# A fused retention and channel-mix kernel: eight key loads on one queue and a new hand-written order

## The chip, the cores and the metric

The kernel runs on one core of a Trainium2 chip. The metric is the device time of one execution in microseconds; the median of the runs is what two kernels are compared by. The engines are named as in the profile: PE (TensorE matrix products; PEld its weight loads), DVE (VectorE), ACT (ScalarE), POOL (GpSimd), SP (SyncE). ACTq, SPq and POOLq are the sequencers of those engines, which also issue DMAs.

## What is computed

Two layers, one after the other, for 4 batches, 8 heads, 768 positions and head dimension 64. The first is a recurrent retention layer with a decay per head:

```python
gamma = 1.0 - 2.0 ** (-5.0 - np.arange(H))
for t in range(S):
    state = gamma * state + einsum('bhd,bhe->bhde', k[:, :, t], v[:, :, t])
    y[:, :, t] = scale * einsum('bhd,bhde->bhe', q[:, :, t], state)
```

Its result, heads side by side (512 values for each position), is the x of the second layer, a channel mix of each position with the one before it:

```python
xk = mu_k * x + (1.0 - mu_k) * x_prev
xr = mu_r * x + (1.0 - mu_r) * x_prev
k = np.maximum(xk @ w_k, 0.0)            # 512 -> 1024
v = k * k @ w_v                          # 1024 -> 512
r = 1.0 / (1.0 + np.exp(-(xr @ w_r)))    # 512 -> 512
return (r * v).astype(np.float32)
```

Inputs and output are float32.

## The kernel before

The positions are cut into 24 chunks c of 128 (six to a batch) for the retention layer and into 12 blocks m of 256 (three to a batch, chunks 2m and 2m+1) for the channel mix. The work is written as pieces, and a long string, ORDER, names every piece in the order in which the program is emitted. There is no other scheduler: each engine runs its own pieces in the order of that string and waits at each for what it needs. The kernel's loop is only this:

```python
for piece in ORDER.split():
    name, *args = piece.split(".")
    pieces[name](*map(int, args))
```

The pieces of chunk c, with the engine that runs them:

- q.c, k.c, v.c: loads of one chunk, 256 KB of float32 in the source. q and v are cast to float16 on the way and always stand in POOL's queue. k stays float32, and its queue is the c-th entry of LOADED_BY, or SP from chunk 8 on.
- ks: the scaling of k by powers of the decay. ks.0.0, ks.0.1, ks.1.0, ks.1.1 (pairs 0 and 1, one chunk each) run on the engine that SCALED_BY names; ks.2 to ks.11 scale two chunks at once on POOL.
- T.c: transposes of q and ks on PE (16 products). TC.c: their copy to float16 on ACT.
- A.c: scores on PE. M.c.0, M.c.1: the causal mask on DVE.
- S.c: update of the state on PE. SE.c: its copy, on ACT for even c, on DVE for odd c.
- Y.c: the chunk's result on PE. YE.c: its decay and copy into xT on DVE.

The pieces of block m: dx.m, the difference to the previous position (on DVE for blocks 0 and 1, there written dx.m.0 and dx.m.1; on POOL for the others); xk.m.j and xr.m.j, the mixtures, on DVE; G.m.g, a quarter of the product with w_k, on PE, and K.m.g, relu and square, on ACT; R.m.t, the product with w_r, on PE, and RS.m.t, the sigmoid, on ACT; V.m.t.p, halves of the product with w_v, on PE; O.m.t, the last product, on DVE; out.m.t, the store, on SP. wk.0, wk.1, wr, wv.0, wv.1 load the weights (1 MB of float32 each, cast to float16) and muk, mur the two mixing vectors; pw.0 and pw.1 make tables of decay powers on DVE.

Chunks are loaded into tiles of two chunks each. There are five such tiles for q, five for v and two for k, so that k.4 can only be loaded when chunks 0 and 1 have been scaled, k.6 after chunks 2 and 3, k.8 after ks.2, and so on. The two choices that the change touches beside ORDER are used here:

```python
def load_k(c):
    eng = getattr(nc, LOADED_BY[c] if c < len(LOADED_BY) else "sync")
    load(k, K32, "k32", F32, eng, c)

eng = nc.gpsimd if c is None else getattr(nc, SCALED_BY[2 * n + c])
if eng is nc.scalar:
    for h in range(H):
        eng.activation(out=KS[n][:, c, h], in_=K32[n][:, c, h], func=AF.Copy, scale=gk[:, c, h : h + 1])
else:
    w = gk[:, e, :, None].to_broadcast([P, e.stop - e.start, H, D])
    eng.tensor_tensor(out=KS[n][:, e], in0=K32[n][:, e], in1=w, op=ALU.mult)
```

Of the kernel before, what the change touches and what calls it, by code (L numbers as in the profile page):

```python
# [28 lines left out]
M.7.1 K.1.3 S.6 xk.2.2 V.0.0.0 q.11 M.7.0 SE.6 Y.6 xk.2.0 q.9 V.0.1.1 xk.2.3 xr.2.0 V.1.0.1 q.8
xk.2.1 V.0.0.1 xr.2.1 v.8 O.1.0 Y.7 YE.6 out.1.0 G.2.2 k.13 YE.7 T.9 k.10 O.0.1 dx.3 S.7 k.11 TC.9  # L30
T.8 SE.7 k.12 G.2.3 TC.8 O.0.0 G.2.0 v.9 xr.2.2 K.2.2 xr.2.3 A.9 A.8 v.10 M.9.1 V.1.1.0 K.2.0
xk.3.2 q.12 S.8 xk.3.3 V.1.1.1 xk.3.1 K.2.3 q.10 xk.3.0 G.2.1 O.1.1 q.13 SE.8 G.3.1 M.8.1 ks.5
K.2.1 M.9.0 G.3.2 M.8.0 R.2.0 K.3.2 xr.3.2 ks.6 k.14 S.9 Y.9 k.15 SE.9 T.11 Y.8 YE.9 TC.11 G.3.3
YE.8 v.11 k.17 RS.2.0 T.10 xr.3.0 out.0.1 A.11 dx.4 k.16 TC.10 S.10 M.11.1 V.2.0.0 M.11.0 SE.10
G.3.0 xr.3.1 q.15 K.3.3 xk.4.2 A.10 xr.3.3 V.2.0.1 v.12 xk.4.3 K.3.0 M.10.0 T.12 v.13 R.2.1 xk.4.0
TC.12 q.14 xk.4.1 T.13 M.10.1 K.3.1 Y.11 q.23 xr.4.1 G.4.3 YE.11 q.16 RS.2.1 Y.10 xr.4.3 TC.13
V.2.1.0 YE.10 G.4.1 K.4.3 dx.5 A.13 A.12 K.4.1 M.13.0 V.3.1.0 ks.7 M.13.1 S.12 V.2.1.1 O.2.0 SE.12
M.12.1 G.4.0 out.2.0 ks.8 O.2.1 G.4.2 K.4.0 xr.4.0 out.2.1 S.13 k.19 T.14 q.21 T.15 k.20 xk.5.1
V.3.0.0 k.21 TC.15 M.12.0 v.20 out.0.0 R.3.0 xr.4.2 xr.5.1 v.14 Y.13 xr.5.2 RS.3.0 Y.12 q.17 YE.13
V.3.0.1 TC.14 xr.5.3 v.15 V.3.1.1 YE.12 K.4.2 T.16 xk.5.3 dx.6 V.4.1.0 SE.13 TC.16 O.3.0 R.3.1  # L40
xk.5.0 V.4.1.1 v.19 RS.3.1 xk.5.2 A.15 O.3.1 A.14 R.4.1 M.14.1 ks.10 M.15.1 G.5.1 RS.4.1 M.14.0
R.4.0 xk.6.2 G.5.2 v.18 k.22 RS.4.0 xk.6.3 k.18 xk.6.0 S.14 v.16 xk.6.1 T.17 SE.14 V.4.0.0 O.4.1
q.18 K.5.1 M.15.0 out.4.1 S.15 Y.14 q.19 out.3.0 SE.15 G.5.3 out.1.1 K.5.2 YE.14 G.6.0 xr.6.2
TC.17 xr.6.3 G.5.0 K.5.3 A.16 A.17 M.16.0 V.4.0.1 K.5.0 ks.9 M.16.1 G.6.1 M.17.1 S.16 xr.5.0 K.6.1
G.6.3 v.23 xr.6.0 Y.15 xr.6.1 K.6.0 v.17 Y.16 YE.15 R.5.0 YE.16 K.6.3 dx.7 R.6.1 M.17.0 SE.16
V.5.0.0 O.4.0 v.21 xk.7.3 RS.5.0 T.21 xk.7.2 S.18 T.18 q.20 xk.7.0 SE.18 T.19 V.5.0.1 q.22 TC.18
G.6.2 v.22 O.5.0 TC.19 xr.7.3 S.19 out.5.0 Y.17 RS.6.1 xk.7.1 k.23 R.5.1 SE.19 TC.21 out.3.1 R.6.0
xr.7.2 K.6.2 YE.17 G.7.2 xr.7.1 dx.8 G.7.1 K.7.2 A.19 A.18 RS.6.0 V.6.0.0 M.18.0 ks.11 RS.5.1
M.18.1 G.7.3 K.7.1 M.19.0 T.20 xk.8.2 V.5.1.0 TC.20 xk.8.3 xr.7.0 G.7.0 M.19.1 V.6.0.1 K.7.0
xk.8.0 A.20 A.21 M.20.0 R.7.1 K.7.3 M.21.0 V.5.1.1 RS.7.1 xk.8.1 M.21.1 S.20 Y.18 SE.20 G.8.0  # L50
O.6.0 M.20.1 Y.19 R.7.0 O.5.1 YE.18 out.5.1 G.8.1 RS.7.0 xr.8.3 K.8.0 Y.20 YE.19 V.7.1.0 xr.8.1
dx.9 K.8.1 xr.8.2 G.8.3 G.8.2 K.8.3 V.6.1.0 xr.8.0 K.8.2 YE.20 Y.21 S.21 xk.9.1 V.7.1.1 xk.9.0
xr.9.2 V.6.1.1 YE.21 T.23 xk.9.2 dx.10 V.8.0.0 O.7.1 TC.23 O.6.1 R.8.0 out.7.1 SE.21 out.6.1 T.22
RS.8.0 out.4.0 V.8.1.0 xk.10.0 TC.22 out.6.0 xk.10.3 R.8.1 xk.9.3 xr.10.1 A.22 RS.8.1 A.23 M.22.1
V.8.1.1 M.23.1 G.9.0 M.23.0 S.22 xk.10.1 K.9.0 V.7.0.0 O.8.1 G.9.2 xk.10.2 SE.22 xr.9.1 V.7.0.1
xr.10.0 K.9.2 M.22.0 G.9.1 xr.9.0 O.7.0 G.10.0 K.9.1 out.7.0 Y.22 Y.23 K.10.0 V.8.0.1 YE.23 YE.22
G.10.3 O.8.0 G.9.3 K.10.3 xr.10.2 G.10.2 xr.9.3 xr.10.3 K.9.3 dx.11 G.10.1 R.9.1 K.10.1 R.9.0
xk.11.1 RS.9.1 xk.11.0 V.9.1.0 K.10.2 xk.11.3 xr.11.1 V.9.0.0 xk.11.2 RS.9.0 V.9.1.1 V.9.0.1 O.9.1
G.11.2 out.9.1 O.9.0 out.8.0 xr.11.2 R.10.0 K.11.2 out.8.1 xr.11.3 G.11.0 xr.11.0 G.11.3 K.11.0
G.11.1 RS.10.0 V.10.0.0 K.11.3 R.10.1 K.11.1 V.10.0.1 R.11.1 RS.10.1 O.10.0 V.10.1.0 out.10.0  # L60
RS.11.1 V.11.1.0 V.10.1.1 V.11.1.1 O.10.1 V.11.0.0 out.10.1 O.11.1 out.9.0 R.11.0 out.11.1
V.11.0.1 RS.11.0 O.11.0 out.11.0
"""


# [1 line left out]
def kernel(  # L67
# [102 lines left out]
    def load(x, tiles, name, dt, eng, c):  # L170
        n, i = divmod(c, 2)
        if n not in tiles:
            tiles[n] = (ldk if dt is F32 else ld).tile([P, 2, H, D], dt, name=name)
# [2 lines left out]
        eng.dma_start(out=tiles[n][:, i], in_=src)  # L176
# [299 lines left out]
```

## Time and profile before

| | |
|---|---|
| median of 7 runs | 168.34 us (167.9 to 168.59) |
| the profiled execution's own time | 169.47 us |
| its span, first to last instruction | 167.7 us |
| PE busy | 143.8 us (86%) |
| DVE busy | 123.8 us (74%) |
| ACT busy | 103.9 us (62%) |
| POOL busy | 89.3 us (53%), its DMA issues included |
| mean of 16 DMA engines | 131 GB/s, 21.96 MB |

All times inside the profile are of that one profiled execution, counted from its first instruction. The page gives busy time by engine, the same in 40 slices of the span (a digit is tenths), the queues, the chain of work that ended last, and the costliest groups of instructions. In a timeline, a line is: start in us, duration in us, engine, source line, operation, output and inputs, count, and in brackets how long the engine had been idle before it and what released it. In a table of stages, a line is: the stage, its length, busy time of PE, PEld, DVE, ACT and POOL with the number of instructions, the granted PE clock (1 is full), the share of DMA, and GB/s. In the chain, a line is: start, duration, and what the chain went through in that time. For a single load the trace gives the start of the issue and the time from there to its landing.

### The profile page before, as it was taken

The numbers are of one execution on the slowest core, as the hardware profiler recorded it, in microseconds if no ns is written. First come the engines' busy times: TensorE is split into PE (matmuls) and PEld (weight loads), VectorE is DVE, ScalarE is ACT, GpSimd is POOL, SyncE is SP. The second block draws the span as 40 slices with busy tenths as digits, with TensorE's granted clock in tenths as the row PEclk, the third lists the DMA queues.
The fourth block names the chain that finished last, engine by engine and source line by source line (L and its number), as shares of the span: only waits on it lengthen the run. The fifth ranks groups of instructions, "written<-read, shape, count | busy, mean of one in ns | idle before, by whom it ended". The sixth has DMA issues, their size and how long they took to land.

```text
span 167.7 us, 5592 instructions
## 1 busy us (share of the span) xinstructions
PE 143.8 (86%) x2448; PEld 108.5 (65%) x2448; DVE 123.8 (74%) x233; ACT 103.9 (62%) x178; POOL 89.3 (53%) x81
## 2 busy tenths in 40 slices
PE   0055854779999999999999989999999999999990
PEld 0044734678758797768668877876886689768540
DVE  2099791998498989969999896869999695551131
ACT  3035602858852979986735986987493577938510
POOL 7996009956494989979959189362044000400000
PEclk9999985899999999999999999999999999999999
DMA  4999994999999999995997999960102401013142
GB/s 46 211 162 158 180 176 106 194 180 187 163 68 198 211 160 173 238 125 157 191 194 101 190 183 76 151 155 4 48 18 100 154 0 66 4 50 140 66 167 86
DMA packets 78505, 21.96 MB, mean 131 GB/s; under 512 B 72464, under 2 KB 75152, under 8 KB 78480
## 3 DMA queue, kind: packets, MB, share of 16 engines
q0 software_dynamic: 52880, 9.97, 72.0%
q1 hardware_dynamic: 20384, 10.58, 23.4%
q10 hardware_dynamic: 5216, 1.05, 3.8%
q8 instruction: 19, 0.31, 0.8%
q14 instruction: 6, 0.05, 0.1%
HBM read 24.22 MB, written 6.29 MB: 182 GB/s over the span
## 4 chain that ended last, share of the span: by engine, by line
PE 71%; DMA 19%; POOL 6%; issue 1%; DVE 0%; ACTq 0%; SPq 0%; POOLq 0%; ACT 0%; DVEq 0%
PE pV L167 24%; PE pZ L167 21%; PE pR L167 12%; DMA k<-in_k_dram 6%; PE pT L212 5%; DMA v<-in_v_dram 5%; DMA wk<-in_moe_w_k_dram 4%; DMA q<-in_q_dram 3%; PE pA L223 3%; PE pY L286 3%; POOL ks L200 2%; PE pY L167 2%; POOL v L176 2%; POOL k L176 2%; PE pS L256 1%
## 5 line engine op out<-in xcount | busy, mean ns | idle before, releaser
L167 PE MATMUL pZ<-xk,wk 128*64 128x256 f16 x768 | 47.2, 274 | 1.9 <-DMA wk<-in_moe_w_k_dram 1.9
L167 PE MATMUL pV<-wv,k 128*64 128x512 f16 x384 | 47.6, 380 | 0.0
L167 PEld LDWEIGHTS <-wk 128*64 128x64 f16 x768 | 42.0, 111 | 6.2 <-DMA wk<-in_moe_w_k_dram 2.1
L216 ACT COPY qkT<-pT 128x1024 f16<-128x1024 f16 x24 | 24.0, 1012 | 28.3 <-PE pT L212 28.2
L314 POOL TENSOR_TENSOR dx<-xT 128x1024 f32<-128x1024 f32 x10 | 19.5, 1946 | 34.8 <-DVE xT L297 20.8
L232 DVE TENSOR_TENSOR a2t<-pA,c_sb 128x512 f16<-128x512 f32 x48 | 31.0, 684 | 7.7 <-PE pA L223 7.6
L345 ACT ACTIVATE kr<-pZ 128x512 f32<-128x512 f32 x48 | 28.5, 593 | 12.4 <-PE pZ L167 12.1
L346 ACT ACTIVATE k<-kr 128x512 f16<-128x512 f32 x48 | 30.2, 630 | 1.5
L200 POOL TENSOR_TENSOR ks<-k,csm_sb 128x1024 f16<-128x1024 f32 x10 | 20.0, 2003 | 19.8 <-DMA k<-in_k_dram 12.5
L167 PEld LDWEIGHTS <-k 128*64 128x64 f16 x384 | 20.1, 110 | 14.3
L324 DVE SCALAR_TENSOR_TENSOR xk<-dx,muk,xT 128x256 f16<-128x256 f32 x48 | 25.5, 565 | 2.2 <-POOL dx L314 2.1
L375 DVE SCALAR_TENSOR_TENSOR osb<-pV,rsb 128x512 f32<-128x512 f32 x24 | 16.4, 687 | 13.8 <-PE pV L167 5.2
L324 DVE SCALAR_TENSOR_TENSOR xr<-dx,mur,xT 128x256 f16<-128x256 f32 x48 | 26.1, 576 | 0.0
L167 PE MATMUL pR<-wr,xr 128*64 128x512 f16 x192 | 24.0, 380 | 0.0
L176 POOL DMA_DIRECT2D v<-in_v_dram x24 | 22.1, 926 | 0.8 <-POOLq L460 0.8
L297 DVE TENSOR_TENSOR xT<-pY,gy_sb 128x512 f32<-128x512 f32 x24 | 16.1, 687 | 8.2 <-PE pY L286 8.1
L359 ACT ACTIVATE rsb<-pR 128x512 f32<-128x512 f32 x24 | 13.9, 592 | 13.1 <-PE pR L167 12.4
L176 POOL DMA_DIRECT2D q<-in_q_dram x24 | 21.6, 922 | 0.0
L256 PE MATMUL pS<-v,ks 128*64 128x64 f16 x160 | 6.5, 205 | 10.7 <-DVE ks L200 9.1
L167 PEld LDWEIGHTS <-xr 128*64 128x64 f16 x192 | 10.8, 110 | 7.3
L256 PEld LDWEIGHTS <-ks 128*64 128x64 f16 x160 | 6.0, 119 | 12.3 <-DVE ks L200 9.1
L212 PE MATMUL pT<-c_sb,ks 128*64 128x128 f16 x192 | 11.0, 243 | 2.8 <-POOL ks L200 2.8
(32 smaller groups left out, 115.6 us busy)
## 6 DMA issues: line engine op xcount, KB each, us to landing
out_dram<-osb SPq DMA_DIRECT2D x24, 256.0 KB, 2.5
k<-in_k_dram SPq DMA_DIRECT2D x16, 256.0 KB, 5.5
v<-in_v_dram POOLq DMA_DIRECT2D x24, 128.0 KB, 6.0
q<-in_q_dram POOLq DMA_DIRECT2D x24, 128.0 KB, 6.1
k<-in_k_dram POOLq DMA_DIRECT2D x4, 256.0 KB, 5.4
k<-in_k_dram ACTq DMA_DIRECT2D x4, 256.0 KB, 7.1
wk<-in_moe_w_k_dram POOLq DMA_DIRECT2D x2, 512.0 KB, 8.7
wv<-in_moe_w_v_dram POOLq DMA_DIRECT2D x2, 512.0 KB, 11.5
```

The costliest lines, as they stand in the source:

```text
L167: nc.tensor.matmul(out[r], lhsT=lhsT[:, r], rhs=rhs, skip_group_check=True, **kw)
L176: eng.dma_start(out=tiles[n][:, i], in_=src)
L200: eng.tensor_tensor(out=KS[n][:, e], in0=K32[n][:, e], in1=w, op=ALU.mult)
L212: nc.tensor.transpose(PT[c][r, i, h // 2, :], heads(src, c, h, 1), ident)
L216: nc.scalar.copy(out=QKT[c], in_=PT.pop(c))
L232: nc.vector.tensor_tensor(out=A2[c][:, hp], in0=PA[c][hp], in1=causal[:, None, :].to_broadcast([P, NJ, C]), op=ALU.mult,)
L297: nc.vector.tensor_tensor(out=xT[b][:, :, col : col + C], in0=PY.pop(c), in1=gy[:, c % 2], op=ALU.mult)
L314: eng.tensor_tensor(out=DX[m][:, :, r], in0=xcur[:, :, r], in1=xprev[:, :, r], op=ALU.subtract)
L324: nc.vector.scalar_tensor_tensor(out=dst[m][:, j], in0=DX[m][:, j], scalar=mu[:, j : j + 1], in1=xprev[:, j], op0=ALU.mult, op1=ALU.add,)
L345: nc.scalar.activation(out=kr, in_=PZ.pop((m, g)), func=AF.Relu)
L346: nc.scalar.activation(out=K2[m][:, 2 * g : 2 * g + 2], in_=kr, func=AF.Square)
L375: nc.vector.scalar_tensor_tensor(out=osb, in0=PV.pop((m, tb)), scalar=1.0 / (KSC * KSC), in1=RS.pop((m, tb)), op0=ALU.mult, op1=ALU.mult,)
```

## The change

Two tuples change and the whole order string is replaced. The fourth of the four early scalings, ks.1.1, goes from ACT to DVE; the loads k.4 to k.7 go from ACT's queue to POOL's. The set of pieces is the same, and no piece's arithmetic changes. In the new order, keys come ahead of the first v loads; the second half of w_k (wk.1) is issued ahead of ks.2 and the first half (wk.0) behind it; the tables of decay powers come ahead of the first scaling; G.0.2 and G.0.3 precede G.0.0 and G.0.1; k.7 and k.6 stand behind wr; q.9 stands ahead of ks.3. The order of later pieces differs throughout. The diff, cut to the opening of the order:

```diff
-SCALED_BY = ("vector", "vector", "vector", "scalar")
-LOADED_BY = ("gpsimd", "gpsimd", "gpsimd", "gpsimd", "scalar", "scalar", "scalar", "scalar")
+SCALED_BY = ("vector", "vector", "vector", "vector")
+LOADED_BY = ("gpsimd", "gpsimd", "gpsimd", "gpsimd", "gpsimd", "gpsimd", "gpsimd", "gpsimd")

 ORDER = """
-muk v.0 k.1 k.0 q.0 k.3 v.1 ks.0.0 v.3 ks.0.1 S.0 T.0 pw.0 q.1 v.4 TC.0 k.2 SE.0 A.0 pw.1 q.3 S.1
-M.0.0 T.1 M.0.1 v.2 TC.1 SE.1 Y.0 q.2 k.4 YE.0 A.1 ks.1.1 q.5 ks.1.0 M.1.0 q.4 M.1.1 S.2 wk.0 k.5
-dx.0.0 Y.1 SE.2 T.3 YE.1 TC.3 dx.0.1 T.2 xk.0.0 TC.2 A.3 M.3.1 mur xk.0.1 A.2 k.6 S.3 xk.0.2 k.7
-ks.2 M.2.0 M.3.0 M.2.1 Y.3 wk.1 xk.0.3 k.8 T.4 SE.3 Y.2 k.9 TC.4 wr YE.2 T.5 q.6 TC.5 S.4 dx.1.0
-G.0.0 v.5 YE.3 SE.4 G.0.1 dx.1.1 q.7 K.0.0 A.4 xk.1.3 wv.0 A.5 xr.0.1 K.0.1 xk.1.2 G.0.3 xk.1.0
-xk.1.1 G.0.2 xr.1.2 K.0.3 xr.1.3 G.1.3 xr.1.1 K.0.2 xr.0.0 G.1.0 xr.0.3 xr.0.2 G.1.1 xr.1.0 K.1.0
-M.4.1 R.0.0 M.4.0 ks.3 K.1.1 R.1.1 M.5.1 G.1.2 M.5.0 RS.1.1 v.6 RS.0.0 T.6 Y.4 TC.6 wv.1 Y.5 YE.4
-T.7 ks.4 YE.5 R.0.1 TC.7 R.1.0 K.1.2 dx.2 A.6 A.7 M.6.1 V.0.1.0 RS.0.1 M.6.0 RS.1.0 V.1.0.0 v.7
+muk k.1 k.0 q.0 pw.0 k.2 ks.0.0 ks.0.1 v.0 pw.1 T.0 TC.0 S.0 v.1 SE.0 A.0 q.1 S.1 ks.1.0 M.0.0
+M.0.1 k.3 SE.1 T.1 Y.0 TC.1 q.3 ks.1.1 A.1 v.4 k.4 YE.0 M.1.0 M.1.1 T.3 v.2 q.2 TC.3 Y.1 A.3 T.2
+TC.2 dx.0.0 YE.1 dx.0.1 xk.0.0 q.4 A.2 mur M.3.0 S.2 SE.2 k.5 M.3.1 M.2.0 M.2.1 v.3 q.5 S.3 xk.0.1
+Y.3 xk.0.3 wk.1 ks.2 Y.2 YE.3 T.5 T.4 YE.2 SE.3 xk.0.2 wk.0 wr k.7 S.4 dx.1.0 TC.4 TC.5 dx.1.1
+xk.1.0 k.6 v.5 SE.4 G.0.2 xk.1.1 G.0.3 xr.1.2 xk.1.3 q.6 q.7 wv.0 xk.1.2 xr.1.0 xr.0.1 xr.1.1
+xr.1.3 xr.0.3 A.4 v.6 k.9 xr.0.0 K.0.2 A.5 K.0.3 G.0.1 G.0.0 G.1.2 K.0.1 K.0.0 M.4.1 xr.0.2 G.1.1
+G.1.0 K.1.1 R.1.0 R.1.1 K.1.0 q.9 ks.3 M.5.1 M.5.0 wv.1 R.0.0 Y.5 M.4.0 YE.5 Y.4 K.1.2 RS.1.0 YE.4
+T.6 G.1.3 T.7 RS.1.1 TC.6 A.6 R.0.1 TC.7 A.7 k.8 ks.4 dx.2 v.7 M.6.0 q.8 M.7.1 xk.2.3 v.8 RS.0.1
...
```

Behind that, POOL's order of loads and of its own work is now: q.11 q.10 dx.3 v.9 q.13 v.10 ks.5 q.15 q.12 v.11 v.21 ks.6 dx.4 v.13 v.12 v.20 v.18 q.16 q.14 v.14 dx.5 ks.7 ks.8 q.23 v.15 q.18 q.22 q.17 v.17 dx.6 q.20 v.16 q.21 q.19 v.19 ks.9 ks.10 dx.7 dx.8 and so on. SP's order begins k.9 k.8 out.0.1 k.10 k.11 k.12 k.13 out.1.1.

More of the change, by code (lines that the diff above doesn't have):

```diff
@@ L29 @@
[L29 to L62, printed above, removed]
+muk k.1 k.0 q.0 pw.0 k.2 ks.0.0 ks.0.1 v.0 pw.1 T.0 TC.0 S.0 v.1 SE.0 A.0 q.1 S.1 ks.1.0 M.0.0
+M.0.1 k.3 SE.1 T.1 Y.0 TC.1 q.3 ks.1.1 A.1 v.4 k.4 YE.0 M.1.0 M.1.1 T.3 v.2 q.2 TC.3 Y.1 A.3 T.2
@@ new lines @@
+q.11 xk.2.2 xk.2.1 xk.2.0 q.10 RS.0.0 M.6.1 V.1.1.0 S.6 V.0.1.0 K.1.3 xr.2.3 M.7.0 V.1.0.0 T.9
+G.2.0 Y.6 V.0.1.1 YE.6 SE.6 xr.2.1 O.0.1 out.0.1 Y.7 V.1.0.1 YE.7 xr.2.2 TC.9 T.8 S.7 SE.7 K.2.0
+TC.8 V.0.0.0 O.1.0 G.2.2 xr.2.0 K.2.2 A.9 k.10 dx.3 v.9 A.8 V.0.0.1 k.11 M.8.0 k.12 xk.3.1 M.8.1
+q.13 G.2.1 O.0.0 K.2.1 G.2.3 Y.8 S.8 K.2.3 YE.8 M.9.0 v.10 ks.5 V.1.1.1 R.2.0 M.9.1 xr.3.2 SE.8
+T.11 xk.3.0 R.2.1 xk.3.3 xk.3.2 Y.9 RS.2.0 k.13 S.9 YE.9 SE.9 O.1.1 out.1.1 T.10 G.3.0 G.3.3 TC.11
+A.11 q.15 TC.10 A.10 M.11.1 q.12 M.10.0 M.11.0 v.11 M.10.1 V.2.1.0 K.3.3 v.21 G.3.2 k.15 ks.6
@@ new lines @@
+K.3.0 dx.4 k.14 S.10 G.3.1 xk.4.2 k.17 T.13 xk.4.0 xk.4.1 v.13 v.12 k.16 SE.10 Y.10 xr.3.0 xr.4.2
+xk.4.3 xr.3.1 V.2.1.1 RS.2.1 xr.3.3 Y.11 v.20 xr.4.0 T.12 K.3.2 K.3.1 V.2.0.0 YE.10 G.4.3 YE.11
+G.4.1 V.2.0.1 TC.13 v.18 A.13 TC.12 A.12 q.16 K.4.3 O.2.1 M.13.1 K.4.1 O.2.0 G.4.0 S.12 SE.12
+R.3.0 R.3.1 G.4.2 q.14 S.13 M.13.0 M.12.0 M.12.1 v.14 Y.12 dx.5 ks.7 T.15 ks.8 q.23 Y.13 K.4.0
+V.4.1.0 RS.3.0 SE.13 T.16 TC.15 v.15 YE.12 K.4.2 V.3.1.0 xr.4.3 q.18 TC.16 xk.5.0 q.22 T.14
+out.1.0 xk.5.2 V.4.1.1 TC.14 xk.5.3 xk.5.1 YE.13 V.3.1.1 A.15 RS.3.1 xr.4.1 M.15.0 A.14 O.3.1
@@ new lines @@
+R.4.1 G.5.2 M.14.0 q.17 v.17 dx.6 S.14 RS.4.1 O.4.1 R.4.0 q.20 k.18 M.14.1 v.16 out.4.1 RS.4.0
+SE.14 xr.5.3 xk.6.1 q.21 K.5.2 xk.6.0 xr.5.0 V.4.0.0 k.19 xr.5.1 xr.6.3 T.17 V.4.0.1 M.15.1 O.4.0
+k.20 G.5.1 G.5.3 TC.17 S.15 xk.6.3 k.21 G.5.0 xk.6.2 K.5.1 A.16 SE.15 V.3.0.0 Y.15 M.16.1 K.5.0
+M.16.0 G.6.3 xr.6.1 K.5.3 xr.5.2 V.3.0.1 Y.14 G.6.1 K.6.1 xr.6.0 A.17 YE.14 M.17.1 q.19 M.17.0
+K.6.3 R.5.0 v.19 YE.15 V.5.0.0 RS.5.0 ks.9 S.16 out.0.0 ks.10 SE.16 T.18 T.21 Y.16 TC.21 G.6.0
+T.19 O.3.0 TC.18 out.2.0 TC.19 V.5.0.1 S.18 SE.18 YE.16 xr.6.2 R.6.1 R.5.1 dx.7 xk.7.3 xk.7.2
@@ new lines @@
+xk.7.1 O.5.0 RS.6.1 Y.17 xr.7.0 T.20 S.19 k.23 R.6.0 TC.20 xr.7.3 RS.5.1 G.6.2 xr.7.2 YE.17 xk.7.0
+A.19 dx.8 SE.19 M.19.1 M.19.0 A.20 M.20.1 out.4.0 K.6.2 G.7.3 K.6.0 M.20.0 V.5.1.0 out.5.0 G.7.0
+Y.19 YE.19 xk.8.3 K.7.3 xk.8.1 RS.6.0 G.7.2 A.18 xr.7.1 K.7.2 A.21 G.7.1 xk.8.0 M.21.0 xk.8.2
+M.18.1 K.7.1 k.22 V.5.1.1 R.7.1 Y.20 out.3.1 G.8.0 M.21.1 ks.11 K.7.0 M.18.0 S.20 V.7.1.0 Y.18
+xr.8.2 RS.7.1 YE.18 G.8.3 SE.20 K.8.0 S.21 YE.20 V.7.1.1 T.23 G.8.1 O.7.1 V.6.0.0 O.5.1 v.23
+out.7.1 dx.9 T.22 G.8.2 K.8.1 xk.9.2 K.8.2 V.6.0.1 xk.9.1 V.6.1.0 Y.21 xr.8.0 O.6.0 V.6.1.1 xr.8.3
@@ new lines @@
+xr.8.1 YE.21 R.7.0 R.8.0 out.5.1 O.6.1 TC.23 SE.21 TC.22 R.8.1 RS.7.0 K.8.3 A.22 RS.8.0 A.23
+V.8.1.0 RS.8.1 xk.9.3 dx.10 xk.10.1 xk.9.0 xr.9.1 G.9.1 M.22.1 v.22 M.23.0 M.23.1 G.9.0 K.9.1
+xk.10.2 xr.9.0 xk.10.0 V.8.0.0 G.9.2 xk.10.3 xr.9.2 K.9.2 V.8.0.1 O.8.0 out.8.0 S.22 xr.10.0 G.9.3
+M.22.0 SE.22 V.8.1.1 Y.23 K.9.3 xr.9.3 K.9.0 out.2.1 Y.22 G.10.1 K.10.1 G.10.2 O.8.1 R.9.1 G.10.3
+YE.22 YE.23 RS.9.1 V.7.0.0 G.10.0 dx.11 K.10.3 K.10.2 out.6.1 R.9.0 xk.11.0 RS.9.0 V.9.1.0 xk.11.1
+xr.10.3 xk.11.3 V.7.0.1 O.7.0 V.9.0.0 V.9.1.1 xk.11.2 G.11.0 K.10.0 G.11.1 xr.11.0 xr.11.3 K.11.0
@@ L63 @@
+K.11.1 xr.10.2 xr.10.1 O.9.1 V.9.0.1 V.10.0.0 R.10.1 out.7.0 G.11.3 out.9.1 O.9.0 G.11.2 RS.10.1
+R.10.0 K.11.2 V.10.0.1 K.11.3 RS.10.0 out.9.0 V.10.1.0 V.11.0.0 xr.11.1 xr.11.2 V.10.1.1 V.11.1.0
+O.10.0 out.3.0 out.6.0 R.11.1 V.11.1.1 out.8.1 O.10.1 R.11.0 out.10.1 RS.11.1 V.11.0.1 out.10.0
+RS.11.0 O.11.1 O.11.0 out.11.1 out.11.0
 """
```

## Prediction

> **What bounds the kernel now.** I read the page's rows in 40 slices first, for where TensorE is not full.
>
> ```profile
> PE   0055854779999999999999989999999999999990
> DVE  2099791998498989969999896869999695551131
> POOL 7996009956494989979959189362044000400000
> PEclk9999985899999999999999999999999999999999
> DMA  4999994999999999995997999960102401013142
> ```
>
> A slice is 4.2 us. PE is thin up to slice 8 (about 34 us) and full until the last slice. In slices 4 and 5 POOL is at 0 and in slice 6 DMA drops to 4 and the clock to half: whatever is wrong is there. The waits of the whole span agree: after 34.61 PE has a single listed wait, of 0.72 us. So the span is 34.6 us of opening, 128.8 us of full PE (34.61 to 163.45) and 4.2 us of tail. An order can shorten the opening; afterwards it can only avoid making holes.
>
> The chain of waits says what ends the opening:
>
> ```profile
> 14.42 0.37 ACTq L176
> ...
> 15.12 10.06 DMA k<-in_k_dram
> ...
> 25.35 1.85 POOL ks L200
> 27.20 7.37 DMA wk<-in_moe_w_k_dram
> 34.57 0.04 issue
> 34.61 4.56 PE pZ L167 x80
> ```
>
> k.5, issued by ACT at 15.12, lands at 25.2; only then can POOL scale chunks 4 and 5 (ks.2), and behind ks.2 in POOL's order stands wk.1, the second half of w_k, which lands at 34.6 and lets PE go on. POOL's timeline shows the queue standing:
>
> ```profile
> 14.49 0.88 POOL L424 DMA_DIRECT2D wk<-in_moe_w_k_dram  x1
> 25.35 1.90 POOL L200 TENSOR_TENSOR ks<-k,csm_sb 128x1024 f16<-128x1024 f32 x1 [9.98 <-DMA k<-in_k_dram]
> 27.20 0.83 POOL L424 DMA_DIRECT2D wk<-in_moe_w_k_dram  x1
> ```
>
> and PE's timeline shows its two holes, and the one much later:
>
> ```profile
> 27.30 0.64 PE L212 MATMUL pT<-c_sb,ks 128*64 128x128 f16 x8 [2.81 <-POOL ks L200]
> 34.61 4.56 PE L167 MATMUL pZ<-xk,wk 128*64 128x256 f16 x80 [1.94 <-DMA wk<-in_moe_w_k_dram]
> 98.06 0.32 PE L256 MATMUL pS<-v,ks 128*64 128x64 f16 x8 [0.72 <-DMA v<-in_v_dram]
> ```
>
> Busy by stage: between 24 and 29 us the DMA engines have almost nothing queued but k.6 and k.7.
>
> ```profile
> 22.00:24.00 2.00, 1.05 (x28) 0.82 (x28) 2.00 (x4) 0.00 (x0) 0.00 (x0) 0.93 1.23 228
> 24.00:25.00 1.00, 0.49 (x9) 0.25 (x5) 0.99 (x4) 0.00 (x0) 0.00 (x0) 0.50 0.38 79
> 25.00:27.00 2.00, 0.00 (x0) 0.00 (x0) 0.25 (x1) 0.00 (x0) 1.65 (x1) 0.50 0.61 139
> 27.00:29.00 2.00, 1.70 (x32) 1.70 (x34) 0.16 (x1) 1.01 (x1) 2.00 (x4) 0.50 0.17 39
> ```
>
> (Last columns: clock, DMA share, GB/s.) At 228 GB/s those 5 us would have moved 1140 KB; they moved 79 + 2x139 + 2x39 = 435 KB. So about 3 us of transfer time are lost.
>
> **The change, part by part.** *Landing times.* For one load, start of issue plus time to landing: k.1 2.3+4.8 = 7.1, k.0 3.2+5.2 = 8.4, q.0 9.2, k.3 10.5, v.1 11.4, v.3 12.3. In POOL's queue a q or v chunk thus follows its neighbour by 0.87 us and a k chunk by 1.3; a weight half (q.7 40.3, wv.0 43.3) by 2.5 to 3. First load: 1.25+3.8 for v.0; for k.1 I take 5.5. The new POOL order then lands: k.1 5.5, k.0 6.8, q.0 7.7, k.2 9.0, v.0 9.8, v.1 10.7, q.1 11.6, k.3 12.9, q.3 13.7, v.4 14.6, k.4 15.9, v.2 16.8, q.2 17.6, q.4 18.5, k.5 19.8, v.3 20.7, q.5 21.5. Issue doesn't limit: 17 issues of 0.9 end at 16.5. k.4 must wait for the scaling of chunks 0 and 1 (they end near 8.2) and issues at 10.2, so that wait is covered by 2 us; with a late DVE it would hold all behind it.
>
> *k.4 to k.7 from ACT to POOL.* Adds 4 x 0.92 = 3.7 us to POOL, which has 9.98 us of waiting there: free, as long as POOL then waits less. Beside the row (ACT issue 0.37 us, but 8.1 and 10.1 us to landing, against 5.6 to 6.5 for POOL's loads just before) stands the Trainium skill, "DMA: Bandwidth & Descriptors", section "Issuing engines are not separate DMA queues": all issuers share 16 engines, several issuers only save issue time. By it alone the move gains nothing and costs POOL 3.7 us: 168.34 + 3.7 = 172. It leaves out order: in one queue k.5 is 15th, in ACT's it shared with wk.0 and four chunks. I go by the landing rows: 19.8 for 25.2.
>
> *ks.2 and the weights.* ks.2 starts 19.9 (25.35 before), ends 21.9. wk.1 now stands ahead of it (issue 16.4), lands 21.5+2.5, with k.8 and k.9 of SP beginning to share: 24.4. wk.0 issues at 22, lands 27.6 (2.5 at a 0.8 share). Both halves are there at 27.6 against 34.6. Then wr 30.7, k.7 and k.6 34.3, v.5 35.2, q.6 36.0, q.7 36.9, wv.0 39.5 (before: 37.3, 27.3, 39.6, 38.6, 40.2, 43.3). The stream itself gains some 3.5 us, the 3 lost above and a shorter start; the weight gains 7 because it is moved past chunks.
>
> *ks.1.1 on DVE.* One 0.68 us instruction for eight on ACT (2.0 us). DVE's order at that place: SE.1 to 13.05, ks.1.1 to 13.75, YE.0, M.1.0, M.1.1 to 15.75. Y.1 waits for it by 0.7, and YE.1, dx.0.1 follow; T.3 needs it at 13.75 and q.3 is there at 13.7. The 2.6 us of gy powers, which stood after the first scaling (9.6 to 12.1), move before it, where DVE waits for k.0. Sum: about nothing on the path.
>
> *PE up to the weights*, at the slow rate of the opening (T 0.86, A 0.6, Y 0.85): T.0 8.0, S.0 9.85 (v.0), A.0 10.2, T.1 11.65 (q.1), Y.0 12.5, A.1 13.6, T.3 14.2, Y.1 15.8 (M.1), T.2 17.65 (q.2), A.2 19.6, S.3 20.75, Y.3 21.5, Y.2 22.3, T.5 and T.4 23.2 to 24.9, S.4, then G.0.2 and G.0.3 from 25.3, A.4, A.5. At 28.0 all that PE had done by 34.61 is done, with G.0.2/G.0.3 for G.0.0/G.0.1, and wk.0 is there. DVE at that point: dx.1 ends 26.5, so xk.1 28.7 for G.1.2 at 29.7, xr to about 33.
>
> *The rest.* The remaining PE pieces are the same set, so 28.0 + 128.8 = 156.8 against 163.45: 6.6 us less. Adding the rows of PE, POOL and DVE along the new order I get these places to give back:
> - clock: half rate could last to about 30 instead of 28: 0 to 1, take 0.5.
> - T.6 (36.4 with that) needs ks.3. POOL: in the program each POOL DMA waits for the landing of the eighth before it, so q.9 waits for wr (30.7), ks.3 waits for k.6 (34.3) and ends 36.3; the k part of T.6 is due about 0.2 after its q part. 0 to 1.5, take 0.5. Behind ks.3 wait wv.1, ks.4, dx.2 (39 to 41), v.7, q.8; q.8 lands 45.9 for T.8 at 46.
> - Loads later. Before, slack of first use over landing between 50 and 98 us was 0.1 to 3 us, so PE may move only as far as the loads do. POOL, walked on without holes, issues q.17 near 76; 6 us on it lands at 82 to 83 for T.17 at about 82. xk or xr now and then takes 2.0 us instead of 0.47 beside a POOL operation (32.62 us), as before. 0 to 3, take 0.8.
> SP's out.0.1 stands between k.8 and k.10, as out.1.0 did; k.10 goes about 6 us earlier. The tail has the same last pieces (R.11.0, V.11.0.1, O.11.0, out): 4.2.
>
> Sum: -6.6 + 1.8 = -4.8. The profiled execution was 169.47 (span 167.7, 1.8 around it) and the median 168.34 lies 1.1 below; I subtract from the median: **163.5**, a span of 162.9.
>
> **The rivals.**
> *No give-back:* 168.34 - 6.6 = 161.7. For: PE work is never short in the new order. Against: the slack rows above.
> *The stream decides:* PE starts 6.6 earlier but the loads only 3.5, and PE has to wait the difference out in holes like that of 98.06. It keeps the stream's 3.5 less one more such hole of 0.7: 168.34 - 2.8 = 165.5. For: DMA stands at 9 in nearly every slice up to 25, and three more q/v chunks than before stand ahead of v.16 (3 x 0.87). Against: the stream was also thin from 45 to 50 us (66 GB/s in the stages), where q.9 is already in and q.8 comes 7 us earlier.
> *POOL becomes the bound (slower):* from dx.2 (39) to v.19 (85) POOL is planned without a hole, and dx.3 to dx.6 stand in its order ahead of 3 to 7 loads each. dx waited 20.8 us for xT before, up to 7.8 at once. Each us that YE is late delays all loads behind it. Before, q.17 landed at 89.4 and T.17 used it at 90.1; if it lands past 89 the whole gain is gone, and at 91 the time is 168.34 + 2 = 170.3. It takes about 7 us of such waits.
> That the change does nothing is excluded: the written order is POOL's order.
>
> **How the numbers follow.** My case 0.45 (162 to 164.8), no give-back 0.15, the stream 0.23, equal within 0.2% 0.03, slower 0.14. About 0.2% is what a measurement of this kernel can tell from no change. Faster 0.83, same 0.03, slower 0.14. The range takes in the first three and leaves out the slower case and some of the fast end: 160.9 to 167.2.
>
> **What would show it.** Right: ks.2 starts at 19.5 to 21; the second w_k half lands by 28.5; PE's last wait of the opening ends at 28 to 29; no GB/s hole between 24 and 29; PE's work ends near 158.6. Wrong in the opening: k.5 landing after 23, or a wait of PE for DVE or ACT between 28 and 36. Wrong later: PE waits in sum above 3 us between 35 and 100, for v, q or ks.

## The result and the profile after

| | before | after |
|---|---|---|
| median | 168.34 us (31 runs, 167.42 to 169.31) | 165.65 us (12 runs, 164.08 to 169.78) |
| the profiled execution's own time | 169.47 us | 164.97 us |
| its span | 167.7 us | 163.2 us |
| PE is full from, and ends at | 34.61, 163.45 us | 28.96, 158.66 us |

The ratio is 0.9822 (0.9797 to 0.9847): about 3.0 us faster. The medians differ by 2.7 us, and the two profiled executions by more, 4.5 us. A median counts all executions of a kernel and a ratio only those within 1.5% of the fastest one; a profile is of a single execution, and where that was a long one for its kernel, its own time stands beside it.

The page of the new kernel, its rows in 40 slices of 4.1 us:

```profile
PE   0158579999999999999999989999999999999980
DVE  6559789954889789878799659877759954573320
POOL 7999299449969799999995080830406004000000
PEclk9999999999999999999999999999999999999999
DMA  3999999999999999999999961450030531027042
```

PE is at 9 from slice 6 (24.5 us) on, where it was from slice 9 (37.7 us; the slices count from 0). The hole of DMA in slice 6 is gone, and so is the clock's drop. POOL's one thin place in the opening is slice 4 (16 to 20 us). POOL's timeline of the new kernel shows why:

```profile
16.24 0.90 POOL L424 DMA_DIRECT2D wk<-in_moe_w_k_dram  x1
20.78 1.90 POOL L200 TENSOR_TENSOR ks<-k,csm_sb 128x1024 f16<-128x1024 f32 x1 [3.64 <-issue]
22.63 0.82 POOL L424 DMA_DIRECT2D wk<-in_moe_w_k_dram  x1
...
33.26 0.88 POOL L176 DMA_DIRECT2D q<-in_q_dram  x1 [2.99 <-DMA wr<-in_moe_w_r_dram]
```

ks.2 starts at 20.78, where it started at 25.35; POOL waited 3.64 us for it, not 9.98. The profile names no releaser here ("issue"), but k.5 lands at 20.65, just ahead, as it landed at 25.18 ahead of 25.35 before. wk.1 (the load at 16.24) is issued before ks.2, wk.0 (22.63) behind it. PE's timeline of the new kernel, end of the opening and every later wait of some size:

```profile
28.13 0.90 PE L223 MATMUL pA<-qkT 64*128 64x128 f16 x16
28.96 4.56 PE L167 MATMUL pZ<-xk,wk 128*64 128x256 f16 x80
...
36.83 0.41 PE L286 MATMUL pY<-a2t,v 128*64 128x128 f16 x8 [0.50 <-DMA v<-in_v_dram]
...
96.49 0.41 PE L212 MATMUL pT<-c_sb,ks 128*64 128x128 f16 x8 [0.69 <-POOL ks L200]
```

The group of 80 products starts at 28.96 behind A.4 and A.5 with no wait at all; afterwards PE waits 0.50 us for v.5 and 0.69 us for a ks. Busy time by stage in the new kernel (columns as before: length, PE, PEld, DVE, ACT, POOL, clock, DMA share, GB/s):

```profile
20.00:25.00 5.00, 4.07 (x78) 3.84 (x80) 4.04 (x7) 0.77 (x3) 4.22 (x4) 1.00 1.02 154
25.00:30.00 5.00, 4.93 (x96) 4.45 (x94) 4.90 (x12) 3.90 (x7) 5.00 (x7) 1.00 1.21 198
```

154 and 198 GB/s stand where the kernel before had 39 to 139 between 24 and 29 us, and the clock is 1.00 where it was 0.50. In the chain of waits no weight is left:

```profile
13.63 2.76 DMA k<-in_k_dram
...
17.21 3.57 issue
...
25.93 10.85 DMA v<-in_v_dram
```

The 7.37 us of w_k are not on it. It runs through v.5's 10.85 us. The 2.76 us are not the whole of k.5, which took 7.02 us from issue to landing: the rest of that time stands in the chain as the 3.57 us ahead of ks.2.

### The profile page after: what moved, and what is told of

The parts are those of the page before. It is cut to its first block, busy times and chain, and to the rows that moved or that the text cites. A ratio compares the mean times of both kernels' runs of the same rounds, so it can differ in the third digit from the quotient of the medians.

```text
span 163.2 us, 5583 instructions
## 1 busy us (share of the span) xinstructions
PE 144.6 (89%) x2448; PEld 108.7 (67%) x2448; DVE 116.7 (71%) x234; ACT 101.7 (62%) x170; POOL 91.2 (56%) x85
## 4 chain that ended last, share of the span: by engine, by line
PE 64%; DMA 14%; POOL 12%; issue 4%; DVE 2%; SPq 1%; POOLq 0%; DVEq 0%
PE pV L167 23%; PE pZ L167 19%; PE pR L167 10%; DMA k<-in_k_dram 8%; DMA v<-in_v_dram 7%; PE pT L212 4%; POOL k L176 4%; PE pA L223 3%; PE pY L286 3%; POOL q L176 3%; POOL v L176 2%; PE pY L167 2%; POOL ks L200 2%; DVE osb L375 1%; SPq L176 1%
## 5 line engine op out<-in xcount | busy, mean ns | idle before, releaser
L167 PE MATMUL pZ<-xk,wk 128*64 128x256 f16 x768 | 48.0, 273 | 0.0
L167 PEld LDWEIGHTS <-wk 128*64 128x64 f16 x768 | 41.0, 110 | 3.5
L200 POOL TENSOR_TENSOR ks<-k,csm_sb 128x1024 f16<-128x1024 f32 x10 | 19.1, 1919 | 12.7 <-DMA k<-in_k_dram 7.9
L324 DVE SCALAR_TENSOR_TENSOR xk<-dx,muk,xT 128x256 f16<-128x256 f32 x48 | 21.9, 496 | 2.7 <-POOL dx L314 2.4
L324 DVE SCALAR_TENSOR_TENSOR xr<-dx,mur,xT 128x256 f16<-128x256 f32 x48 | 21.8, 487 | 0.0
L212 PE MATMUL pT<-c_sb,q 128*64 128x128 f16 x192 | 11.0, 243 | 8.2 <-DMA q<-in_q_dram 8.1
L167 PEld LDWEIGHTS <-xr 128*64 128x64 f16 x192 | 10.3, 110 | 7.6
L212 PEld LDWEIGHTS <-q 128*64 128x64 f16 x192 | 8.3, 124 | 10.6 <-DMA q<-in_q_dram 8.7
```

Of the source, the lines that this page charges most:

```text
L167: nc.tensor.matmul(out[r], lhsT=lhsT[:, r], rhs=rhs, skip_group_check=True, **kw)
L212: nc.tensor.transpose(PT[c][r, i, h // 2, :], heads(src, c, h, 1), ident)
L324: nc.vector.scalar_tensor_tensor(out=dst[m][:, j], in0=DX[m][:, j], scalar=mu[:, j : j + 1], in1=xprev[:, j], op0=ALU.mult, op1=ALU.add,)
```

## The experiments

The theory: the gain is the opening's, and it comes from k.5's place in one queue with w_k moved past the scaling. Its rivals: it is the queue alone, or the order alone; the later part of the order; ks.1.1; the clock. The runs of the new kernel also spread more widely than those of before, and the last runs look for that. Each run was measured beside the kernel before on the same chip; on the three chips used for them, the median of before was 168.07 to 169.11 us, which is what stands behind "against". In the diffs, lines of the order are cut to the pieces that move.

**Queue alone.** The kernel before with its old order, eight keys in POOL's queue.

```diff
-LOADED_BY = ("gpsimd", "gpsimd", "gpsimd", "gpsimd", "scalar", "scalar", "scalar", "scalar")
+LOADED_BY = ("gpsimd", "gpsimd", "gpsimd", "gpsimd", "gpsimd", "gpsimd", "gpsimd", "gpsimd")
```

> Only LOADED_BY changes: k.4 to k.7 go to POOL's queue, in the old order, where k.5 stands behind wk.0. Theory A (the gain is the place in the queue, not the queue): k.5 lands at about 24.9 us (25.2 before), ks.2 starts near 25, wk.1 still lands after 33, and the time is 0 to 1 us below before. Rival B (taking the loads off ACT's queue is itself the gain): k.5 lands by 22, the time is 2.5 us or more below before.

Measured: 168.28 against 168.85, ratio 0.998 (0.9943 to 1.0017): no gain that can be told from none. POOL's timeline of this run:

```profile
16.15 1.05 POOL L176 DMA_DIRECT2D k<-in_k_dram  x1
...
24.88 1.90 POOL L200 TENSOR_TENSOR ks<-k,csm_sb 128x1024 f16<-128x1024 f32 x1 [5.59 <-DMA k<-in_k_dram]
26.73 0.81 POOL L424 DMA_DIRECT2D wk<-in_moe_w_k_dram  x1
```

k.5 (the load at 16.15) now stands in POOL's queue, but in its old place, behind q.5, q.4 and the first half of w_k: it lands at 24.80 (25.2 before), and wk.1 is issued at 26.73 (27.20 before). The queue by itself does nothing. It also costs nothing: POOL waits 5.59 us instead of 9.98.

**Queue and three moves.** The old order with k.4 ahead of v.2, k.5 ahead of q.5 and wk.1 ahead of ks.2, in POOL's queue.

```diff
+LOADED_BY = ("gpsimd", "gpsimd", "gpsimd", "gpsimd", "gpsimd", "gpsimd", "gpsimd", "gpsimd")
...
-M.0.0 T.1 M.0.1 v.2 TC.1 SE.1 Y.0 q.2 k.4 YE.0 A.1 ks.1.1 q.5 ks.1.0 M.1.0 q.4 M.1.1 S.2 wk.0 k.5
+M.0.0 T.1 M.0.1 k.4 v.2 TC.1 SE.1 Y.0 q.2 YE.0 A.1 ks.1.1 k.5 q.5 ks.1.0 M.1.0 q.4 M.1.1 S.2 wk.0
...
-ks.2 M.2.0 M.3.0 M.2.1 Y.3 wk.1 xk.0.3
+wk.1 ks.2 M.2.0 M.3.0 M.2.1 Y.3 xk.0.3
```

> The old order with three moves and the one-queue LOADED_BY: k.5 ahead of q.5, k.4 ahead of v.2, wk.1 ahead of ks.2. Theory A: ks.2 starts near 20.5 us, both halves of w_k are there before 29, the full-PE stretch starts 4 to 6 us earlier than 34.6 and the time falls by 2 to 3.5 us, as with the whole change. Rival C (the rest of the new order is needed to use the earlier start): the opening is early but PE then waits for loads between 36 and 100 us for 2 us or more, and the time falls by less than 1 us.

Measured: 166.74 against 168.85, ratio 0.9857 (0.9808 to 0.9906). POOL's timeline, PE's timeline and one stage of this run (lines are one lower than in the other kernels):

```profile
20.25 2.35 POOL L199 TENSOR_TENSOR ks<-k,csm_sb 128x1024 f16<-128x1024 f32 x1 [0.38 <-DMA k<-in_k_dram]
```

```profile
32.29 4.56 PE L166 MATMUL pZ<-xk,wk 128*64 128x256 f16 x80
```

```profile
24.00:28.00 4.00, 3.23 (x64) 3.00 (x62) 3.31 (x8) 0.89 (x1) 4.00 (x5) 0.51 1.25 195
```

Three moves bring k.5 from 24.80 to 20.18 and wk.1 to 29.02. PE then waits for no weight. Its big group starts at 32.29, 2.3 us earlier than before and not the 4 to 6 expected: in this execution PE's own work ahead of it runs at half clock (0.51 in that stage). That this makes the median longer is not shown, as the two of its six executions with a mean clock below 0.99 (166.32 and 167.15) lie among the others (165.6 to 168.6). PE ends at 160.86, 2.6 us earlier than before; the new kernel, which has no such stage, ends 4.8 earlier. In time the three moves bring 2.4 us of the new kernel's 3.0, and the intervals overlap. The three were not run one by one.

**Order alone.** The new order with the old queues.

```diff
-LOADED_BY = ("gpsimd", "gpsimd", "gpsimd", "gpsimd", "gpsimd", "gpsimd", "gpsimd", "gpsimd")
+LOADED_BY = ("gpsimd", "gpsimd", "gpsimd", "gpsimd", "scalar", "scalar", "scalar", "scalar")
```

> The new order with the old LOADED_BY: k.4 to k.7 on ACT. Theory A: k.5 issues on ACT only behind SE.2 (about 21 us), lands at 25 to 27, ks.2 starts 5 to 6 us later than the 20.8 of the new kernel and wk.0 lands after 32: the gain is lost, 168 to 171 us. Rival (the new order alone carries the gain): within 0.7 us of the new kernel, 165 to 166.5.

Measured: 170.28 (167.88 to 173.14) against 168.85, ratio 1.0017 (0.9967 to 1.0066). POOL's timeline and PE's timeline of this run (its profiled execution took 172.18 us):

```profile
24.85 2.31 POOL L200 TENSOR_TENSOR ks<-k,csm_sb 128x1024 f16<-128x1024 f32 x1 [9.50 <-DMA k<-in_k_dram]
```

```profile
27.21 0.64 PE L212 MATMUL pT<-c_sb,ks 128*64 128x128 f16 x8 [5.01 <-POOL ks L200]
34.44 4.56 PE L167 MATMUL pZ<-xk,wk 128*64 128x256 f16 x80 [1.55 <-DMA wk<-in_moe_w_k_dram]
```

Loaded by ACT, k.5 lands at 24.68 in the new order too: ks.2 waits 9.50 us (9.98 before), wk.0 behind it lands at 34.39, and the whole gain is gone. The reason is not the one of before: k.5 took only 4.69 us from issue to landing (10.06 before). It was late because ACT came to issue it only at 19.98, behind its own copies, where POOL issues it at 13.63. So neither the queue alone nor the order alone does it: the order needs a queue whose engine is free to issue early.

**New opening, old rest.** The new order up to the last piece ahead of T.6 (q.9 among them), the old order for the pieces that are left, new queues.

```diff
 R.1.0 R.1.1 K.1.0 q.9 ks.3 M.5.1 M.5.0 wv.1 R.0.0 Y.5 M.4.0 YE.5 Y.4 K.1.2 RS.1.0 YE.4
-T.6 G.1.3 T.7 RS.1.1 TC.6 A.6 R.0.1 TC.7 A.7 k.8 ks.4 dx.2 v.7 M.6.0 q.8 M.7.1 xk.2.3 v.8
+k.8 G.1.3 RS.1.1 RS.0.0 T.6 TC.6 T.7 ks.4 R.0.1 TC.7 dx.2 A.6 A.7 M.6.1 V.0.1.0 RS.0.1 M.6.0
...
```

> The new order up to the piece before T.6 (about 37 us) and from there the old order with what is left; the new queues. Theory A (the opening carries the gain): full PE starts near 29 us as in the new kernel and the time is within 0.7 us of it, 2 to 3.5 us below before. Rival C (the new rest carries part of it): PE waits for loads after 37 us by 1.5 us or more and the time is 1 us or more above the new kernel.

Measured: 166.24 against 168.85, ratio 0.9837 (0.9787 to 0.9887), on the mark of the new kernel's 0.9822. PE's timeline of this run:

```profile
28.94 4.56 PE L166 MATMUL pZ<-xk,wk 128*64 128x256 f16 x80
...
44.73 1.49 PE L166 MATMUL pV<-wv,k 128*64 128x512 f16 x12 [0.47 <-DMA wv<-in_moe_w_v_dram]
```

PE is full from 28.94 and ends at 158.66, the new kernel's numbers, and the waits it has later (0.29, 0.38 and 0.47) are as small. The opening carries the gain.

**Old opening, new rest.** The reverse: old order, queues and scaling up to T.6, then the new order for what is left.

```diff
 M.4.1 R.0.0 M.4.0 ks.3 K.1.1 R.1.1 M.5.1 G.1.2 M.5.0 RS.1.1 v.6 RS.0.0
-T.6 Y.4 TC.6 wv.1 Y.5 YE.4 T.7 ks.4 YE.5 R.0.1 TC.7 R.1.0 K.1.2 dx.2 A.6 A.7
+R.1.0 q.9 wv.1 Y.5 YE.5 Y.4 K.1.2 RS.1.0 YE.4 T.6 T.7 TC.6 A.6 R.0.1 TC.7 A.7 ks.4 dx.2
...
```

> The old order and old queues up to the piece before T.6, then the new order with what is left: the counterpart of the run with the new opening. Theory A (all of the gain is in the opening): full PE starts at 34 to 35 us and the time is that of before within 0.7 us. Rival C (the new rest gives something by itself): 1 us or more below before, with fewer PE waits after 35 us (0.72 us of waiting before).

Measured: 171.76 (169.43 to 174.17) against 169.11, ratio 1.0083 (1.003 to 1.0135). PE's timeline of this run:

```profile
26.73 0.64 PE L212 MATMUL pT<-c_sb,ks 128*64 128x128 f16 x8 [1.88 <-POOL ks L200]
34.13 4.56 PE L167 MATMUL pZ<-xk,wk 128*64 128x256 f16 x80 [1.02 <-DMA wk<-in_moe_w_k_dram]
44.60 0.40 PE L223 MATMUL pA<-qkT 64*128 64x128 f16 x8 [0.66 <-ACT qkT L216]
```

The new rest brings nothing of its own. Behind the old opening it makes a hole of 0.66 at 44.60 and a wait of 1.32 for a ks at 102.22, and the kernel is about 1.4 us slower (0.0083 of 168.34) by the ratio and 2.65 by the medians, where within 0.7 was expected. A second reading matters more below: the opening here is the kernel before's, piece for piece, and its big group starts at 34.13, while in the profile of before it started at 34.61. The same opening differs by 0.5 us from execution to execution: k.5 landed at 24.61 here and at 25.18 there.

**wk.0 ahead of ks.2.** The new kernel with one piece moved.

```diff
-xk.0.3 wk.1 ks.2 Y.2 YE.3 T.5 T.4 YE.2 SE.3 xk.0.2 wk.0 wr
+xk.0.3 wk.1 wk.0 ks.2 Y.2 YE.3 T.5 T.4 YE.2 SE.3 xk.0.2 wr
```

> The new kernel with wk.0 ahead of ks.2 instead of behind it, so that POOL issues it at 17 us and not at 22.6. Both halves of w_k land by 27 (28.7 in the new kernel). If wk.0's landing holds PE at 29 us: full PE starts 1 us or more earlier and the time falls by 0.7 us or more. If PE's own slow work up to A.5 holds it (it ends at 29.03 in the new kernel, just behind the landing): the time stays within 0.4 us.

Measured: 164.82 against 169.11, ratio 0.9741 (0.9682 to 0.9799). wk.0 lands at 27.64 (28.66 in the new kernel), wr at 31.05 (32.97), v.5 at 35.71 (36.79), so the wait for v.5 goes; PE ends at 158.21. PE's big group does not start earlier, though (29.22, against 28.96), and the gain of at least 0.7 us was expected only with an earlier start. The profile shows 0.45 us less of PE's end; the ratio gains more.

**A fuller PE in the opening.** The new kernel with 39 idle products of 128x256 in the holes of PE's opening, written by a new piece D into a PSUM tile that nothing reads, to see whether the clock is what makes its runs spread; and the same with wk.0 ahead of ks.2.

```diff
+    def filler(n):
+        pD = psm.tile([P, 2, TM], F32, name="pD", tag="m")
+        for i in range(n):
+            nc.tensor.matmul(
+                pD[:, 0, :], lhsT=c16[:, 0:P], rhs=c16, start=True, stop=True, skip_group_check=True,
+            )
...
-muk k.1 k.0 q.0 pw.0 k.2 ks.0.0 ks.0.1 v.0 pw.1 T.0 TC.0 S.0 v.1
+muk k.1 k.0 q.0 pw.0 k.2 ks.0.0 ks.0.1 v.0 pw.1 D.16 T.0 TC.0 D.7 S.0 v.1
...
```

> The new kernel with 39 idle products of 128x256 on PE (into a free PSUM buffer, never read) put into the holes of the opening: before T.0, S.0, S.1, A.1, T.2, A.2 and S.3. Theory H (the new kernel's runs spread from 164.1 to 166.2 because its opening ends on a PE still at half clock, for a time that differs from run to run): the clock is full before 20 us, T and Y in the opening take half as long, PE has done A.5 by 27 and waits for wk.0 at 28.7; the spread narrows to under 1 us and the median falls by 0.5 to 1 us. Rival (the spread has another cause): median within 0.3 us or higher by the filler's own time, spread unchanged.

> The filler and wk.0 ahead of ks.2 together. If the stream of loads is what holds PE next (v.5 lands at 36.8 and q.6 at 37.7 in the new kernel, with 0 to 0.5 us of slack): full PE starts near 27 us, but PE then waits 1 to 2 us before Y.5 and T.6, and the time is within 0.5 us of the filler alone. If not: 1.5 us below the filler alone, near 163.

Measured: 165.91 (165.04 to 170.1), ratio 0.9789 (0.9724 to 0.9854), and with wk.0 first 164.84 (163.49 to 167.3), ratio 0.9754 (0.9697 to 0.9812). The second is the 164.82 of wk.0 first alone again, on the same chip: the filler adds nothing and narrows nothing. Two stages of the first of them (profiled execution 170.1 us):

```profile
16.00:20.00 4.00, 1.36 (x29) 0.89 (x30) 3.53 (x6) 0.00 (x0) 1.18 (x2) 1.00 1.99 173
20.00:24.00 4.00, 3.54 (x53) 2.31 (x49) 1.94 (x4) 1.75 (x3) 2.36 (x2) 0.63 0.98 134
```

q.2 came late in that execution, PE waited 2.63 us for it and was busy 1.36 of 4 us, and in the next stage the clock was 0.63 in spite of the filler. The clock is not shown to cause the spread. The filler did not even raise it: the mean granted clock of its six executions is 0.979 to 0.988, while eleven of the new kernel's twelve have 0.993 to 1.000, and those take 164.08 to 166.73 us.

Nor is the clock what the change gains by. The kernel before has a mean clock of about 0.98 in some executions, as in its profile with the stage at half clock, and of about 1.00 in others. Beside the next runs, its four executions with a mean clock of 0.998 or more took 168.02 us on average and its seven with 0.98 or less 168.08; on two other chips the lower clock was 0.4 us ahead and 0.2 behind. And in the run with the old opening and the new rest, the mean clock was 1.000 and the big group still started only at 34.13.

**The new kernel and the one with wk.0 first, side by side.** Both again on one chip, unchanged; the diff is between the two.

```diff
-xk.0.3 wk.1 ks.2 Y.2 YE.3 T.5 T.4 YE.2 SE.3 xk.0.2 wk.0 wr
+xk.0.3 wk.1 wk.0 ks.2 Y.2 YE.3 T.5 T.4 YE.2 SE.3 xk.0.2 wr
```

> The new kernel itself again, with a profile of another execution, as the measure for the three others on the same chip. Theory L (an execution above the first profile's 164.97 us is one whose early loads land later or whose clock rises later): if this one takes 165.5 or more, full PE starts after 29.5 us or PE has waits for loads of 1 us or more behind it. Rival: full PE starts at 29.0 and runs without holes, and the time is lost nowhere that the opening explains.

> The kernel with wk.0 ahead of ks.2 once more, now on the same chip as the new kernel. If wk.0's place is worth something by itself: 0.7 us or more below the new kernel, as the ratios to before suggest (0.974 against 0.982). If that was a difference of chips: within 0.4 us of it.

Measured: the new kernel 166.11 (165.03 to 167.24), ratio 0.9889 (0.9853 to 0.9925); with wk.0 first 164.02 (163.05 to 167.69), ratio 0.9738 (0.9708 to 0.9769). The intervals are apart. This is the version that beats both kernels, by the median about 2.1 us below the new one, by the mean of all six executions of each (164.79 and 166.12) 1.3 us. PE's timeline of the new kernel's second profiled execution (165.65 us, span 163.9):

```profile
29.08 4.56 PE L167 MATMUL pZ<-xk,wk 128*64 128x256 f16 x80
...
37.24 0.41 PE L286 MATMUL pY<-a2t,v 128*64 128x128 f16 x8 [0.79 <-DMA v<-in_v_dram]
```

From k.5 on, the loads of the opening are some 0.3 us later than in the first profile (k.5 21.0, wk.0 28.92, v.5 37.2), the wait for v.5 is 0.79 instead of 0.50, and PE ends at 159.37. The other late wait, for ks.10, grows more, from 0.69 to 1.11 us, because k.21 from SP's queue lands at 95.08 and not at 94.38. Moving wk.0 leaves this one: it is 0.90 in the first profile with wk.0 first and 2.41 in the one with the filler (167.3 us). The new kernel's place for wk.0 leaves v.5 no slack, so a slightly later stream shows; with wk.0 first v.5 lands 1.1 us earlier and PE does not wait for it. That is a reading of single profiles; that it makes the whole difference is not shown.

**ks.1.1 back on ACT.**

```diff
-SCALED_BY = ("vector", "vector", "vector", "vector")
+SCALED_BY = ("vector", "vector", "vector", "scalar")
```

> The new kernel with ks.1.1 back on ACT (eight instructions, 2.0 us, for one of 0.68 on DVE). My step says that it is worth about nothing on the path: within 0.4 us of the new kernel. Rival: T.3 waits for it (ks.1.1 would end 1.3 us later, at 15.1 instead of 13.8), and YE.1, A.3 and what follows move by it: up to 1.3 us slower.

Measured: 165.22 (164.42 to 166.4), ratio 0.9841 (0.9802 to 0.988), beside 0.9889 for the new kernel on the same chip; PE ends at 158.41. The median is 0.9 us below the new kernel's (166.11), where 0.4 either way was expected, but the intervals overlap: the move to DVE is worth nothing that shows.

**Two more keys behind the weights.** wk.0 first, and k.9 and k.8 taken from SP's queue to POOL's, behind q.7, so that SP's queue has nothing to land while wk.0, wr and v.5 do.

```diff
-LOADED_BY = ("gpsimd", "gpsimd", "gpsimd", "gpsimd", "gpsimd", "gpsimd", "gpsimd", "gpsimd")
+LOADED_BY = ("gpsimd", "gpsimd", "gpsimd", "gpsimd", "gpsimd", "gpsimd", "gpsimd", "gpsimd", "gpsimd", "gpsimd")
...
-k.6 v.5 SE.4 G.0.2 xk.1.1 G.0.3 xr.1.2 xk.1.3 q.6 q.7 wv.0
+k.6 v.5 SE.4 G.0.2 xk.1.1 G.0.3 xr.1.2 xk.1.3 q.6 q.7 k.9 k.8 wv.0
```

> wk.0 ahead of ks.2, and k.9 and k.8 in POOL's queue behind q.7 instead of in SP's as soon as ks.2 ends. If the loads of SP that run beside the stream hold up v.5 and q.6: these land 1.5 us or more earlier than the 35.7 and 36.8 of the kernel with wk.0 moved, and the time falls by up to 0.7 us. If PE's own work holds it there: no change, or 0.5 us slower from POOL's two more issues.

Measured: 165.17 (163.24 to 166.48), ratio 0.9819 (0.978 to 0.9858), not better than wk.0 first alone on the same chip: worse by the ratio (0.9738 there), equal by the mean of all six executions (164.92 and 164.79). v.5 lands at 32.76 and q.6 at 33.64, 3 us earlier than with wk.0 first alone, and wk.0 at 26.87. PE's timeline of this run:

```profile
28.91 4.56 PE L167 MATMUL pZ<-xk,wk 128*64 128x256 f16 x80
```

The group still starts at 28.91, 2 us after its weight is there. At that point PE's own work holds the opening, and earlier loads buy nothing that shows.

## Why the prediction was nearly right, and where it was not

Predicted 163.5 us, measured 165.65. The prediction said a span of 162.9 and PE's end near 158.6; the profile of the new kernel says 163.2 and 158.66. By the profile, then, the fall was 4.5 us for 4.8. The medians fell by 2.7, so that the result lies inside the stated range (160.9 to 167.2) but outside the prediction's own case (162 to 164.8).

**The step that failed** is the last one, "I subtract from the median". It noted that the profiled execution of before lay 1.1 us above the median and carried its difference over in full. The profiled execution of the new kernel lay 0.7 us below its own median (164.97 and 165.65). The two together are the 1.8 us between 4.5 and 2.7. A part can be seen: the same old opening ended at 34.13 in another kernel's profile and not at 34.61, and the new opening at 29.08 in a second profile and not at 28.96. By these two the opening gains 5.05 us, not 5.65. The new kernel's later part can be 0.6 longer as well (29.08 to 159.37, 130.3 us, against 129.7): the longer waits for v.5 and ks.10 are 0.7 in sum. Those parts make about 1.2 of the 1.8; where the rest lies no run showed.

**The opening.** Right in its mechanism and near in its sizes: ks.2 at 20.78 (19.9 said), wk.1 at 24.08 (24.4), PE full from 28.96 (28.0, with 0.5 for the clock 28.5). The mis-sized terms stand behind ks.2: k.5 and ks.2 were 0.9 late, so wk.0 landed at 28.66 (27.6), wr at 32.97 (30.7), v.5 at 36.8 (35.2). The 0.5 for half clock was not needed, as the clock stayed at 1.00; wk.0 and A.5, which end at 28.66 and 29.03, took its place. That PE's end came within 0.1 us is luck in part: the full stretch began 0.46 us later than the 28.5 said, and lasted 129.7 where 128.8 and 1.3 to give back make 130.1.

**What is given back.** 1.3 us were put down for T.6 and later loads. T.6 did not wait in the new kernel's profile; v.5 (0.50) and ks.10 (0.69) did, and the full stretch grew from 128.8 to 129.7. The wait of POOL for wr ahead of q.9, which the prediction derived from the program's limit of eight, is there, 2.99 us long. The tail took 4.5 for 4.2.

**The price of POOL.** The rule weighed in the prediction (the Trainium skill, "DMA: Bandwidth & Descriptors", "Issuing engines are not separate DMA queues") would have given 172. With the queue alone the time was 168.28, so the four issues on POOL cost nothing, and the order inside one queue was worth 2.4 us (1 - 0.9857 of 168.34) with three moves. The rule held in its first half: the queue alone gained nothing. It was not ACT's queue as such that made k.5 slow, either. Issued just behind half of w_k, it took 10.06 us on ACT (before) and 8.66 on POOL (queue alone); issued on ACT 5.5 us behind such a half it took 4.69 (order alone).

**ks.1.1 "about nothing":** 0.9841 without it, 0.9889 with it, intervals that overlap. Right as far as these runs can tell.

**The rivals.** The stream's case gave 165.5, the number nearest to the result, but by a mechanism that did not come: PE's waits after the opening were 1.2 us in sum (0.50 + 0.69). POOL as the bound did not come either: q.17 landed at 83.1 and T.17 used it at 83.7. No give-back (161.7) was too good by the 0.9 of the full stretch, the 0.3 of the tail, the later start (28.96 for 28.0) and the 1.8 of the step that failed.

## What to carry to other kernels

In every profile here the loads of one queue landed in the order in which they were issued, so what matters is which small load stands behind which large one. Here moving the keys to POOL's queue was worth something only together with their place in the order, and the order only with a queue whose engine came to the issue in time. Ask of each step ahead of a wait (here a weight's issue behind a scaling) whether it must stand there. A difference of two profiled executions is only as good as the executions are alike (here they lay 0.7% above and 0.4% below their medians); before carrying it to the median, see on which side of its own median each of them lies. When the second is not known yet, take the first one's distance as an error of the forecast, not as a constant.
